# A new instruction order for a one-core attention and GEGLU block, with three of four normalised inputs taken from a transposed copy in DRAM

## The chip, the core and the metric

The kernel runs on one core of a Trainium2 chip. A core has five instruction streams: TensorE (matrix products and transposes; PE in the profile, its weight loads PEld), VectorE (DVE), ScalarE (ACT), GpSimd (POOL) and SyncE (SP), which here issues nearly all DMA transfers. Each stream runs its instructions in the order in which they were written. TensorE writes to PSUM, eight banks of 128 partitions by 512 fp32; VectorE and ScalarE read and write PSUM and SBUF; GpSimd works on SBUF alone. The metric is the device time of one execution in microseconds, median of the runs; lower is better.

## The reference

The input is 2048 tokens of width 512, in four segments of 512 tokens. First comes attention with a compressive memory, 32 heads of width 16, and then a gated feed-forward block of inner width 1376 (cut):

```python
h  = x + _A_ref(_layernorm(x), wq, wk, wv, wo, beta)
h2 = h + _B_ref(_layernorm(h), w_gate, w_up, w_down)
# _A_ref, per head, over the segments s = 0..3:
logits = qs @ ks.T * scale + mask       
a_dot  = softmax(logits) @ vs
a_mem  = phi(qs) @ M / (phi(qs) @ z + 1e-6)   # phi(t) = t+1 if t>0 else exp(t)
o      = g * a_mem + (1 - g) * a_dot     # g = sigmoid(beta)
M, z   = M + phi(ks).T @ vs, z + phi(ks).sum()
# _B_ref
h = gelu(x @ w_gate) * (x @ w_up);  out = h @ w_down
```

The mask is `(ar[:, None] < ar[None, :]) * -1e9` over the 512 positions of a segment. All arithmetic is fp32.

## The kernel before

**Precision.** An fp32 product is made of three products of a fast format: each operand is split into a high and a low part (`split_weight`, `split_wv`, `split_psum`), where ScalarE copies the high part and VectorE or GpSimd subtracts it for the low one, and TensorE forms high by high, high by low and low by high (`SPLIT`).

**The first norm.** `ln1_first` handles segment 0. `ln1(s)` handles segments 1 to 3: it loads four tiles `rows[t]` of 128 tokens by 512 features (line 938) and calls `layer_norm` (736). There the mean and variance of each token come from VectorE (segment 1: `bn_stats`, 761) or ScalarE (segments 2 and 3: two passes with accumulators, 747 and 756). From them follow two factors per token, y (one over the standard deviation) and b (minus mean times y), four columns of 128 tokens each. For segment 1 they come from ScalarE's square root and VectorE's reciprocal (795 to 803), for segments 2 and 3 and the second norm from a short chain of VectorE operations on four columns (809, 811, 814; all of `steps` are recorded at line 778). Then ScalarE normalises the rows in place (805, 818). As projections need features on the partitions, TensorE transposes the rows, 32 instructions of 64 by 64 in two tilings per segment (831, by `sides`, 552, with a small VectorE copy "tock" at 564 between its two phases), and `split_psum` takes the result out of the banks in two parts (ScalarE 867, VectorE 868). The result is `XT[s]`, four pairs of 128 features by 512 tokens.

**Attention.** Work goes in 16 units of eight heads and one segment (`UNITS`: units 0 and 1 are of segment 0, 2 and 3 of segment 1, and so on). `qkv` projects q and k (`project`, 959; `project_first`, 980) and v (`vproj`, 1008 and 1021); transfers scatter q and k to the tiles `stq` and `stk` (1083, 1089). `pass_a` forms scores (1213), and VectorE takes their largest per query under the mask (1223). `pass_b` forms them again, transposed (1271); ScalarE takes the exponential (1277), GpSimd clears what is above the diagonal (1285), and TensorE multiplies by v (1299). `mem` reads the memory (1161, 1181), and `mup` adds to it (1124). `wo_seg` projects the output (1372, 1379).

**Feed-forward.** `ffn` runs the gate and up products by a seven-product scheme over blocks of the normed input (1563), with the gate's function in `geglu` (1581 to 1599). The down product runs transposed with seven products per pair of blocks for most of the inner width (`down7`, 1737 and 1748), and plainly for the rest (`down`, 1631 and 1639). `turned` transposes the first sort through DRAM (718, 722, 1774) and adds them up on GpSimd (1775). In pass 1 `geglu` splits the last whole block, f = 9, on VectorE (1599), other blocks of the plain sort on GpSimd. The very last `down` group of pass 1 writes the output; one of its tiles (s = 1, t = 3) is done in two halves of 256 columns, whose transfers go out on two queues.

**Order.** The instructions are not issued where the functions stand. Each call of `pe`, `act`, `dve`, `pool` or `dma` records an operation (a group of instructions of one engine) with a duration. `Sched.run` walks a list of operation numbers, `ORDER`, found beforehand by a search that used the same durations. It emits each operation in turn, and while it does so keeps a clock per engine, from which it knows at what time buffers come free: a `Pool_` hands out the buffer that has been free longest. So `ORDER` sets the order on every engine, and the durations in the code set only which of several free buffers or banks is given out. All eight PSUM banks form one pool (`banks`, 567).

Of the kernel before, what the change touches and what calls it, by code (L numbers as in the profile page):

```python
# [15 lines left out]
P = 128  # L16
D = 512
# [397 lines left out]
class Sched:  # L415
# [7 lines left out]
    def op(self, eng, dur, prio, fn, ins=(), outs=(), acq=(), lat=None, chain=False,  # L423
# [18 lines left out]
        for v in o.vals:  # L442
            v.users += 1
# [61 lines left out]
def infini_geglu(ctx: ExitStack, tc: tile.TileContext, x, wq, wk, wv, wo, beta,  # L505
# [220 lines left out]
    def layer_norm(prio, rows, dst, off=False, keep=None, acq=None, done=(), behind=(), scratch=None, by_side=False, swap=None):  # L726
# [57 lines left out]
        def z_():  # L784
            return z.t
# [1096 lines left out]
```

## Time and profile before

| | |
|---|---|
| Median of 3 runs | 741.16 us (741.01 to 743.85) |
| The profiled execution: its time, its span | 740.42 us, 738.7 us |
| TensorE clock granted | 1.000 |
| Busy in the span: PE, DVE, ACT, POOL | 719.6, 634.8, 534.0, 523.1 us |
| DMA | 137.32 MB in 100798 packets, mean 186 GB/s |
| First attention products to the last ones | about 24 to 390 us |
| Gate, up and down products | about 390 to 734 us |

A busy time is the union of an engine's instructions; in the two-tile modes of attention several matrix instructions run side by side, so the sum of their durations is larger. A line of a group gives line, engine, operation, what it writes and reads, count, busy time and mean length of one in ns, and then the idle time of the engine just before, with what ended it. In a timeline a row gives start and length in us. In the chain of waits the rows are pieces of the path that ended last.

### The profile page before, as it was taken

What the parts mean: (1) busy time and instruction counts of PE and PEld (TensorE: products, weight loads), DVE (VectorE), ACT (ScalarE), POOL (GpSimd) and SP (SyncE); (2) the same over time, 40 slices, a digit from 0 to 9 for tenths busy, and PEclk for the clock granted to TensorE, in tenths of its full rate; (3) what the DMA queues carried; (4) which work ended last, traced back from release to release, by engine and by line L of the source; (5) the groups of instructions that cost most, each with busy time, mean ns of one, the idle gap of its engine ahead of it and who ended that gap; (6) DMA issues with size and microseconds to landing.
All of it is one profiled execution on the core that took longest, in us unless ns stands there. A gap on an engine that the chain in (4) does not pass through costs nothing.

```text
span 738.7 us, 19243 instructions
## 1 busy us (share of the span) xinstructions
PE 719.6 (97%) x6442; PEld 570.6 (77%) x6442; DVE 634.8 (86%) x1990; ACT 534.0 (72%) x1138; POOL 523.1 (71%) x815
## 2 busy tenths in 40 slices
PE   6999999999999999999999999999999999999996
PEld 5877877777878787777666888888887778888885
DVE  6998889988988888898987665889999999779996
ACT  6789979798685878867867656978787665666341
POOL 6344253554553746778899899998999977698766
PEclk9999999999999999999999999999999999999999
DMA  7754537656666776887856267677574249756767
GB/s 256 204 144 109 131 99 191 183 142 174 170 157 168 193 202 190 210 237 202 212 189 211 74 198 234 214 238 216 185 219 142 71 127 269 247 180 204 220 173 248
DMA packets 100798, 137.32 MB, mean 186 GB/s; under 512 B 18028, under 2 KB 40732, under 8 KB 100700
## 3 DMA queue, kind: packets, MB, share of 16 engines
q1 hardware_dynamic: 100396, 135.71, 63.6%
q8 instruction: 51, 0.84, 0.5%
q10 hardware_dynamic: 304, 0.39, 0.2%
q14 instruction: 47, 0.39, 0.2%
HBM read 70.67 MB, written 39.26 MB: 149 GB/s over the span
## 4 chain that ended last, share of the span: by engine, by line
PE 67%; DVE 11%; issue 3%; POOL 2%; DMA 2%; ACT 2%; SPq 1%; ACTq 0%; DVEq 0%; POOLq 0%
PE bank L1563 23%; PE bank L959 8%; PE bank L1299 7%; PE bank L1737 7%; PE bank L1271 5%; PE bank L1213 4%; PE bank L1379 3%; PE bank L1372 3%; PE bank L1008 3%; DVE row L1748 2%; DVE aside L1223 2%; PE bank L1631 2%; DVE bank L1223 1%; PE bank L1181 1%; DMA t_dram<-row 1%
## 5 line engine op out<-in xcount | busy, mean ns | idle before, releaser
L1277 ACT ACTIVATE row<-bank 128x512 f32<-128x512 f32 x320 | 170.9, 608 | 24.8 <-PE bank L1271 20.3
L1285 POOL TENSOR_SCALAR_AFFINE_SELECT row<-row 128x256 f32<-128x256 f32 (+1 forms) x320 | 107.8, 364 | 96.1 <-ACT row L1277 95.0
L1223 DVE CUSTOM_DVE_ANT_0 aside<-bank,amask 128x256 f32<-128x256 f32 (+2 forms) x384 | 141.1, 419 | 12.4 <-PE bank L1213 6.7
L959 PE MATMUL bank<-slot,slot 64*128 64x512 f32 x720 | 113.5, 403 | 0.3 <-DVE nm L1223 0.2
L1563 PE MATMUL bank<-slot,slot 128*128 128x512 f32 (+1 forms) x366 | 97.3, 390 | 0.0
L1223 DVE CUSTOM_DVE_ANT_0 bank<-bank,amask 128x512 f32<-128x512 f32 x128 | 86.1, 710 | 10.5 <-PE bank L1213 7.5
L1271 PE MATMUL bank<-stq,stk 64*128 64x128 f32 (+3 forms) x512 | 82.1, 337 | 0.8 <-ACT row L1114 0.5
L1299 PE MATMUL bank<-row,vaug 128*32 128x512 f32 (+3 forms) x1024 | 79.0, 436 | 1.8 <-DVE nm L1223 1.2
L1213 PE MATMUL bank<-stk,stq 64*128 64x256 f32 (+3 forms) x512 | 78.9, 326 | 1.7 <-DVE nm L1223 1.1
L1563 PEld LDWEIGHTS bank<-slot,slot 128*128 128x128 f32 (+1 forms) x366 | 67.8, 186 | 15.8 <-ACT stq L1419 0.4
L1748 DVE TENSOR_TENSOR row<-row,bank 128x512 f32<-128x512 f32 x110 | 72.0, 677 | 7.1 <-PE bank L1737 5.6
L959 PEld LDWEIGHTS bank<-slot,slot 64*128 64x128 f32 x720 | 73.3, 185 | 6.0 <-DVE nm L1223 0.7
L1528 POOL TENSOR_TENSOR slot<-row,slot 128x512 fp32r<-128x512 f32 (+3 forms) x60 | 67.1, 1124 | 14.1 <-ACT slot L1526 14.0
L1271 PEld LDWEIGHTS bank<-stq,stk 64*128 64x128 f32 x512 | 55.5, 185 | 15.5 <-DVE nm L1223 3.7
L1213 PEld LDWEIGHTS bank<-stk,stq 64*128 64x128 f32 x512 | 56.1, 185 | 9.6 <-DVE nm L1223 2.4
L1737 PE MATMUL bank<-slot,half 128*128 128x512 f32 x234 | 61.7, 390 | 0.0
L1299 PEld LDWEIGHTS bank<-row,vaug 128*32 128x32 f32 x1024 | 30.0, 109 | 39.2 <-issue 34.1
L1008 PE MATMUL bank<-slot,slot 64*128 64x256 f32 x672 | 53.4, 284 | 0.0
L1570 ACT ACTIVATE vaug<-bank 128x512 f32<-128x512 f32 (+1 forms) x66 | 38.5, 591 | 18.6 <-PE bank L1563 18.5
L1737 PEld LDWEIGHTS bank<-slot,half 128*128 128x128 f32 x234 | 43.8, 188 | 9.6 <-DVE row L1748 0.4
L1223 DVE DVE_READ_ACCUMULATOR2_ANT nm<- 128x1 f32 x512 | 49.9, 97 | 0.0
L1008 PEld LDWEIGHTS bank<-slot,slot 64*128 64x128 f32 x672 | 48.7, 186 | 1.0 <-DVE mb L1138 0.2
(228 smaller groups left out, 1722.2 us busy)
## 6 DMA issues: line engine op xcount, KB each, us to landing
stq<-slot SPq DMA_DIRECT2D x96, 128.0 KB
stk<-slot SPq DMA_DIRECT2D x94, 128.0 KB
row<-x SPq DMA_DIRECT2D x32, 256.0 KB
pv_dram<-row SPq DMA_DIRECT2D x32, 256.0 KB
row<-r_dram SPq DMA_DIRECT2D x28, 256.0 KB
wd_dram<-half SPq DMA_DIRECT2D x28, 256.0 KB
half<-wd_dram SPq DMA_DIRECT2D x28, 256.0 KB
row<-wu SPq DMA_DIRECT2D x20, 256.0 KB
```

The source lines that it names most:

```text
L959: return nc.tensor.matmul(pm[i].t, w[i].t[rows_of(r), wi, dc * P:(dc + 1) * P], XT[s][dc].t[rows_of(r), xi, :], start=(dc, wi, xi, ph) == ...
L1008: return nc.tensor.matmul(pms[n].t[:, 256 * t:256 * t + 256], XT[s][dc].t[rows_of(r), xi, t0:t0 + P], whl[wi].t[rows_of(r), dc // 2, 256 * ...
L1213: nc.tensor.matmul(sa.t[:, c0:c0 + w], sq.t[own, p, i * P:(i + 1) * P], sk.t[own, p, 0:w], start=True, stop=True, tile_position=(64 * a, 0 ...
L1223: nc.vector.tensor_tensor_reduce(out=(sa.t[:, c0:c0 + w] if i > 2 else aside[:, turns[0]:turns[0] + w]), in0=sa.t[:, c0:c0 + w], in1=amask ...
L1271: nc.tensor.matmul(sc.t[:, c0:c0 + D - q0], sk.t[own, p, q0:q0 + P], sq.t[own, p, q0:D], start=True, stop=True, tile_position=(64 * a, 0), ...
L1277: act(w, prio, lambda sc=sc, e=e: nc.scalar.activation(e.t[:, :w], sc.t[:, :w], AF.Exp), [sc, vtab], [e])
L1285: nc.gpsimd.affine_select(v, v, pattern=pat + [[1, P]], compare_op=OP.is_ge, fill=0.0, base=0, channel_multiplier=-1)
L1299: nc.tensor.matmul(pv.t[32 * n:32 * n + 32, kb * P:D], va.t[:, 136 * kb + 17 * j:136 * kb + 17 * j + 32], e.t[:, lo:lo + D - kb * P], star ...
L1528: pool(0.14 + 2.13e-3 * (hi - lo), prio, lambda: nc.gpsimd.tensor_tensor(v.t[:, 1, :hi - lo], r.t[:, lo:hi], v.t[:, 0, :hi - lo].bitcast(F ...
L1563: nc.tensor.matmul(dst.t[:w], v.t[:, wi, c0 + j * w:c0 + (j + 1) * w], b[bk][j].t[:, xi, :], start=first and j == 0 and n == 0, stop=j == ...
L1737: nc.tensor.matmul(dst[u].t, ws[a].t[0][:, wi, P * u:P * u + P], h[bk].t[:, xi], start=first and m == 0, stop=m == 2, skip_group_check=True)
L1748: dve(D, prio, lambda u=u, acc=acc: nc.vector.tensor_tensor(acc.t, acc.t, src[u].t, op=OP.add), [src[u]], [acc])
```

## The change

**A new list.** `ORDER` is replaced throughout; it has 5322 entries in place of 5308.

**Turns.** The planner's clock gets a rule for banks: where ScalarE and VectorE both read one bank, one starts only after the other has ended. It enters the planned times, and nothing is emitted for it.

**The first norm of segments 1 to 3.** `layer_norm` is called with `seg=s` and, once y and b are there, calls the new `across`. y and b (4 columns of 128 tokens) are written to a small DRAM tensor as 512 single elements each; after both have landed, each is read back as one row of 512 spread over all 128 partitions. A transposed copy of x, which the host lays out as one more input, is loaded in four tiles of 128 features by 512 tokens. GpSimd multiplies each by the first factor row and adds the second, ScalarE copies the high part, and GpSimd subtracts for the low part. The normalising pass of ScalarE, the transposes, "tock" and `split_psum` of these segments go. The rows are still loaded, for mean and variance.

**Small parts.** In the chain of four-column operations the value z is kept in the bank that holds the other scratch values, with one added copy to SBUF, for every norm with scratch; two planned durations change with it. For the block f = 9 `geglu` writes its product into a bank that it has just read, and the two halves of its split are read from there. The split of the last output tile into two halves is undone.

```diff
@@ Op recording and Sched.run
+        o.reads = [v for v in ins if v.pool is not None and v.pool.turns] if eng in ("ACT", "DVE") else []
...
+            for v in o.reads:
+                for e, end in v.read.items():
+                    if e != o.eng:
+                        at = max(at, end + LAT[e][o.eng])
...
+            for v in o.reads:
+                v.read[o.eng] = end
@@ infini_geglu
-    PD = PX = PYZ = PA = PB = PPV = Pool_(banks)
+    PD = PX = PYZ = PA = PB = PPV = Pool_(banks, turns=True)
...
+    n_dram = dram.tile([NSEG, 2, D], F32, name="n_dram")
@@ layer_norm
         def z_():
-            return z.t
+            return sc.t[:, 12:16] if scratch else z.t
+
+        def third():
+            if scratch:
+                nc.vector.tensor_copy(z.t, z_())
+            nc.vector.scalar_tensor_tensor(u_(), z.t, -10.0 / 3.0, z_(), op0=OP.add, op1=OP.mult)
...
-            dve(280, prio, inv, [z, mv], [y, b])
-            for t in range(4):
+            dve(910, prio, inv, [z, mv], [y, b])
+            for t in range(4) if seg is None else []:
...
+        if seg is not None:
+            return across(prio, seg, y, b, dst)
@@ new
+    def across(prio, s, y, b, dst):
+        vn, ab = Val(), [Val(PROW), Val(PROW)]
+        for i, v in enumerate((y, b)):
+            dma(prio, lambda i=i, v=v: nc.sync.dma_start(n_dram[s, i].rearrange("(t p) -> p t", p=P), v.t),
+                [v], [vn], kb=100, dur=0.5, chain=True)
+        for i, r in enumerate(ab):
+            src = n_dram[s, i]
+            dma(prio, lambda src=src, r=r: nc.sync.dma_start(r.t, bass.AP(
+                tensor=src.tensor, offset=src.offset, ap=[[0, P], [1, D]])), [vn], [r])
+        for dc in range(ND):
+            r = Val(PROW)
+            dma(prio, lambda dc=dc, r=r: nc.sync.dma_start(r.t, xt_in[s * ND + dc]), [], [r])
+            for i, o in enumerate((OP.mult, OP.add)):
+                pool(1.24, prio, lambda i=i, o=o, r=r: nc.gpsimd.tensor_tensor(r.t, r.t, ab[i].t, op=o), [ab[i]], [r])
+            act(D, prio, lambda dc=dc, r=r: nc.scalar.activation(dst[dc].t[:, 0], r.t, AF.Copy), [r], [dst[dc]],
+                src=0.092)
+            pool(1.24, prio, lambda dc=dc, r=r: nc.gpsimd.tensor_tensor(
+                dst[dc].t[:, 1], r.t, dst[dc].t[:, 0].bitcast(F32), op=OP.subtract), [r], [dst[dc]])
@@ geglu
+            if f == 9 and hh:
+                o = g_ if s else u_
...
-            act(D, prio, lambda: nc.scalar.activation(hh.t[:w, 0], e.t[:w], AF.Copy), [e], [hh],
-                src=0.09)
+            act(D, prio, lambda: nc.scalar.activation(hh.t[:w, 0], o.t[:w], AF.Copy), [o], [hh],
+                src=0.067 if f == 9 else 0.09)
...
-                hh.t[:w, 1], e.t[:w], hh.t[:w, 0].bitcast(F32), op=OP.subtract), [e], [hh])
+                hh.t[:w, 1], o.t[:w], hh.t[:w, 0].bitcast(F32), op=OP.subtract), [o], [hh])
@@ down
-                parts = 2 if (p, fl, s, t) == (1, groups[-1], 1, 3) else 1
...
+                a = ACC[4 * s + t]
+                pm = Val(PD)
```

More of the change, by code (lines that the diff above doesn't have):

```diff
@@ L58, with __init__ @@
 ORDER = [
[271 rows of a table removed]
[271 rows of a table added]
 ]
 class Pool_:
-    def __init__(self, tiles, fifo=False, then=None):
+    def __init__(self, tiles, fifo=False, then=None, turns=False):
+        self.turns = turns
         self.free = [(0.0, i, t) for i, t in enumerate(tiles)]
@@ L391, in __init__ @@
         self.users = 0
+        self.read = {}
         self.until = 0.0
@@ L399 @@
     __slots__ = ("eng", "dur", "lat", "fn", "prio", "vals", "preds", "succ", "n", "ready", "idx", "head", "tail",
-                 "mode")
+                 "mode", "reads")
 LAT = {
@@ L505, in infini_geglu @@
 def infini_geglu(ctx: ExitStack, tc: tile.TileContext, x, wq, wk, wv, wo, beta,
-                 wg, wu, wd, wdp, out):
+                 wg, wu, wd, xt_in, wdp, out):
     nc = tc.nc
@@ L724, in blocks_out, with layer_norm @@
                     q.t[32 * a:32 * a + 32].rearrange("p (b x) -> p b x", b=4)), [q], [v], kb=70, dur=0.5, chain=True)
-    def layer_norm(prio, rows, dst, off=False, keep=None, acq=None, done=(), behind=(), scratch=None, by_side=False, swap=None):
+    def layer_norm(prio, rows, dst, off=False, keep=None, acq=None, done=(), behind=(), scratch=None, by_side=False, swap=None, seg=None):
         bn, mv = Val(PBN), Val(PMV)
@@ L784, in z_ @@
         def z_():
-            return z.t
+            return sc.t[:, 12:16] if scratch else z.t
[3 more added lines that the diff above has]
+            nc.vector.scalar_tensor_tensor(u_(), z.t, -10.0 / 3.0, z_(), op0=OP.add, op1=OP.mult)
         steps = [(stt(u_, v_, 1.0, y_, OP.mult, OP.mult), [v, y], [u]),
-                 (stt(z_, u_, 1.0, y_, OP.mult, OP.mult), [u, y], [z]),
-                 (stt(u_, z_, -10.0 / 3.0, z_, OP.add, OP.mult), [z], [u]),
+                 (stt(z_, u_, 1.0, y_, OP.mult, OP.mult), [u, y], [sc if scratch else z]),
+                 (third, [sc], [u, z]) if scratch else (third, [z], [u]),
                  (stt(y_, u_, 5.0, y_, OP.add, OP.mult), [u, y], [y]),
@@ L810, in layer_norm @@
             for f, ins, outs in steps:
-                dve(4, prio, f, ins, outs)
+                dve(200 if f is third and scratch else 4, prio, f, ins, outs)
         if off:
@@ L940, in ln1 @@
         layer_norm(prio, rows, XT[s], off=s > 1, done=[Val()] if s < 2 else [],
-                   behind=[*XT[0], *XL] if s == 1 else [], scratch=PPV if s < 2 else PD, by_side=True)
+                   behind=[*XT[0], *XL] if s == 1 else [], scratch=PPV if s < 2 else PD, by_side=True, seg=s)
         if s < 2:
@@ L1590, in geglu @@
             o = g_ if s and f % 2 and by7(p, f) else e
+            if f == 9 and hh:
+                o = g_ if s else u_
             dve(D, prio, lambda: nc.vector.scalar_tensor_tensor(
-                o.t[:w], r.t[:w], 0.5, u_.t[:w], op0=OP.mult, op1=OP.mult), [u_] if o is r else [u_, r], [o])
+                o.t[:w], r.t[:w], 0.5, u_.t[:w], op0=OP.mult, op1=OP.mult), [v for v in (u_, r) if v is not o], [o])
             HH[p, f, s] = hh or o
@@ L1620, in down, with dn @@
             for t in range(4):
-                parts = 2 if (p, fl, s, t) == (1, groups[-1], 1, 3) else 1
-                a, W_ = ACC[4 * s + t], D // parts
-                halves = [slice(i * W_, (i + 1) * W_) for i in range(parts)]
-                pms = [Val(PD) for _ in halves]
+                a = ACC[4 * s + t]
+                pm = Val(PD)
                 for f in fl:
-                    def dn(t=t, f=f, s=s, pm=None, cs=None):
+                    def dn(t=t, f=f, s=s, pm=pm):
                         w = FW[f]
@@ L1630, in dn @@
                         for n, (hi, wi) in enumerate(SPLIT):
-                            nc.tensor.matmul(pm.t[:, cs], HH[p, f, s].t[:w, hi, t * P:(t + 1) * P],
-                                             v.t[:w, wi, cs], start=f == fl[0] and n == 0,
+                            nc.tensor.matmul(pm.t, HH[p, f, s].t[:w, hi, t * P:(t + 1) * P],
+                                             v.t[:w, wi, :], start=f == fl[0] and n == 0,
                                              stop=f == fl[-1] and n == 2)
-                    for pm, cs in zip(pms, halves):
-                        pe(3 * mm(W_), prio, lambda dn=dn, pm=pm, cs=cs: dn(pm=pm, cs=cs),
-                           [HH[p, f, s], FWS[p, f]["d"]], [pm])
-                for i, (pm, cs) in enumerate(zip(pms, halves)):
-                    to = Val(PC) if parts > 1 else a
-                    dve(W_, prio, lambda a=a, pm=pm, cs=cs, to=to: nc.vector.tensor_tensor(
-                        to.t[:, cs], a.t[:, cs], pm.t[:, cs], op=OP.add), [pm, a], [to])
-                    if fl in ((10,), (8, 9)):
-                        n, q = 8 * p + 4 * s + t, nc.scalar if i else nc.sync
-                        dst = g_dram[n * P:n * P + P] if fl == (10,) else tokens(out, p, s, t, cs)
-                        dma(prio, lambda to=to, cs=cs, q=q, dst=dst: q.dma_start(
-                            dst, to.t[:, cs]), [to], [GD[n]] if fl == (10,) else [])
+                    pe(3 * mm(D), prio, dn, [HH[p, f, s], FWS[p, f]["d"]], [pm])
+                dve(D, prio, lambda a=a, pm=pm: nc.vector.tensor_tensor(a.t, a.t, pm.t, op=OP.add), [pm], [a])
+                if fl in ((10,), (8, 9)):
+                    n = 8 * p + 4 * s + t
+                    dst = (g_dram if fl == (10,) else out)[n * P:n * P + P]
+                    dma(prio, lambda a=a, dst=dst: nc.sync.dma_start(dst, a.t), [a],
+                        [GD[n]] if fl == (10,) else [])
     def tokens(x, p, s, t, cs=slice(0, D)):
@@ L1870 @@
         "wd": np.ascontiguousarray(np.asarray(inputs["B_w_down"])),
+        "xt": np.ascontiguousarray(np.asarray(inputs["A_x"]).reshape(NSEG, D, ND, P).transpose(0, 2, 3, 1).reshape(
+            NSEG * ND, P, D)),
         "wdp": np.ascontiguousarray(np.asarray(inputs["B_w_down"])[:2 * BY7[0] * P].reshape(-1, 4, 2, 2, 32).transpose(
```

542 rows, old and new, of the table ORDER are left out of this document.

## Prediction

> **What bounds the kernel now.** I read the totals and the chain of waits first, then the busy time of each engine by stage, then the groups of instructions that the diff touches.
>
> ```profile
> span 738.7 us, 19243 instructions
> PE 719.6 (97%) x6442; PEld 570.6 (77%) x6442; DVE 634.8 (86%) x1990; ACT 534.0 (72%) x1138; POOL 523.1 (71%) x815
> PE 67%; DVE 11%; issue 3%; POOL 2%; DMA 2%; ACT 2%; SPq 1%; ACTq 0%; DVEq 0%; POOLq 0%
> ```
>
> ```profile
> core 0: us, PE busy (x) PEld busy (x) DVE busy (x) ACT busy (x) POOL busy (x), PEclk, DMA share, GB/s
> ...
> 24.00:60.00 36.00, 35.21 (x445) 29.52 (x447) 33.89 (x161) 30.39 (x73) 14.86 (x37) 1.00 0.57 155
> ...
> 146.00:182.00 36.00, 35.68 (x454) 26.67 (x447) 30.99 (x130) 31.25 (x72) 19.38 (x52) 1.00 0.59 158
> 24.00:390.00 366.00, 359.92 (x4793) 278.64 (x4793) 322.46 (x1371) 294.67 (x660) 208.06 (x469) 1.00 0.65 174
> 390.00:700.00 310.00, 309.53 (x1381) 250.52 (x1378) 264.26 (x503) 213.16 (x425) 273.48 (x290) 1.00 0.62 192
> 700.00:738.70 38.70, 32.91 (x148) 26.36 (x146) 31.34 (x71) 10.67 (x18) 25.46 (x21) 1.00 0.71 216
> ```
>
> From the chain of waits, one piece of the feed-forward stage:
>
> ```profile
> 402.37 12.32 PE bank L1563 x54
> ```
>
> From 390 to 700 us TensorE idles 0.5 us of 310, and a 512-column product takes 12.32 / 54 = 0.228 us, a steady cadence. No order makes this stage shorter; the change neither adds nor removes a product there. So what the change can win lies in attention (24 to 390 us), where TensorE idles 366 - 359.9 = 6.1 us, VectorE is busy 88% (94% from 24 to 60 us) and ScalarE 81%, and in the last 39 us. In attention TensorE and VectorE must both lose work for the time to fall. GpSimd has 158 us free there.
>
> **What the change removes and adds.** The rows of the work that segments 1 to 3 lose, and of a GpSimd operation of the kind that they gain:
>
> ```profile
> L831 PE MATMUL bank<-ident,row 64*128 64x64 f32 x160 | 10.5, 229 | 0.7 <-DVE row L822 0.5
> L868 DVE TENSOR_TENSOR slot<-bank,slot 128x512 fp32r<-128x512 f32 x17 | 11.1, 683 | 0.0
> L867 ACT ACTIVATE slot<-bank 128x512 fp32r<-128x512 f32 x17 | 9.8, 624 | 0.0
> L564 DVE COPY tock<-bank 128x1 f32<-128x1 f32 x48 | 7.4, 155 | 6.1 <-PE bank L1181 2.7 <-PE bank L959 2.1 <-PE bank L831 0.5
> L805 ACT ACTIVATE row<-row,ln,ln x4: 797/809/817, 23.4 to 26.6; 128x512 f32<-128x512 f32 x4
> L818 ACT ACTIVATE row<-row,ln,ln 128x512 f32<-128x512 f32 x16 | 12.8, 816 | 0.2 <-DVE ln L814 0.2
> L1338 POOL TENSOR_TENSOR row<-row,row 128x512 f32<-128x512 f32 x16 | 20.6, 1291 | 3.9 <-DMA row<-r_dram 3.9
> ```
>
> The 160 transposes serve five norms of 32; three go: 96 / 160 x 10.5 = **6.3 us of TensorE**. VectorE loses 12 x 0.683 + 6 x 0.155 = 9.1 us. ScalarE loses the normalising pass, 4 x 0.81 + 8 x 0.816 = 9.8 us; its 12 copies of 0.624 us stay, with a row as source. GpSimd gains 36 operations of 1.291 us, **46.5 us**. SP's queue gains 24 transfers: 12 loads of x and 6 spreads of 256 KB, and 6 writes of 512 single elements. All three engines that are nearly full in attention shed work, so I count TensorE's 6.3 us in full, **-6.3**. The bounds: -9.1 where VectorE sets the pace, 0 where the transposes only filled a wait of TensorE.
>
> **The order.** It is a new list throughout: of 1215 TensorE groups only some 150 keep their neighbour. Its "turns" change only the time that the planner assigns, and so which bank or buffer is handed out; no instruction gets a wait from them. What can be counted in the lists: changes between the tilings of TensorE (row halves, column quarters, whole) fall from 91 to 83, four visits fewer to the column tiling. What a visit costs is bounded by one with nearly no columns in it:
>
> ```profile
> 129.08 0.46 PE L1124 MATMUL bank<-vaug,row 128*32 128x34 f32 x32
> 129.47 0.46 PE L831 MATMUL bank<-ident,row 64*128 64x64 f32 x8
> ```
>
> 0.39 us from start to start, columns included, so four visits are worth 0 to 1.6 us; I take -0.8. For the rest of the reordering the trace gives bounds only: it can at best win the 6.1 us of idle TensorE and might lose as much; I take 0 and keep both ends.
>
> **Short operations that wait for GpSimd.** The norm's step that multiplied z by z from two SBUF operands, beside the same step with a bank operand; then three pieces at 380 and 728 us:
>
> ```profile
> L778 DVE SCALAR_TENSOR_TENSOR bank<-bank,ln 128x4 f32<-128x4 f32 x18 | 3.0, 168 | 0.4
> L778 DVE SCALAR_TENSOR_TENSOR bank<-ln 128x4 f32<-128x4 f32 x6 | 2.5, 419 | 0.2
> ```
>
> ```profile
> 380.41 1.18 DVE bank L778
> ```
>
> ```profile
> 727.01 0.75 DVE L1639 TENSOR_TENSOR row<-row,bank 128x256 f32<-128x256 f32 x2 [0.46 <-POOL row L1775]
> 728.89 1.38 DVE L1599 TENSOR_TENSOR slot<-row,slot 128x512 fp32r<-128x512 f32 x1 [1.13 <-ACT slot L1596]
> 730.32 3.25 PE L1631 MATMUL bank<-stq,slot 128*128 128x512 f32 x13 [0.63 <-DVE slot L1599]
> 732.32 2.05 DVE L1639 TENSOR_TENSOR row<-row,bank 128x512 f32<-128x512 f32 x3 [0.26 <-PE bank L1631]
> ```
>
> Four elements take 0.168 us with a bank operand, 0.419 on average without, and 1.18 at 380 us, on the chain. There the change saves 1.18 - 0.17 less the copy that it adds (0.17 by the same row): **-0.8**. The copy costs the five other norms about as much as it saves. At 728.89 the last subtraction reads two SBUF operands and takes 1.38 us; TensorE waits for it. From a bank it takes 0.68 (the L868 row): **-0.7**. Undoing the split of one output tile costs nothing: its halves ran at 727.0, and three whole tiles follow at 732.3, where the end hangs; were it last in the new list, half an addition (0.34) would come back. The new list ends in a GpSimd addition and one output tile, as the old one does.
>
> [...]
>
> **The new wait: the factors of segment 1.** Today:
>
> ```profile
> 0.00:20.00 20.00, 13.68 (x98) 11.69 (x99) 13.69 (x38) 12.12 (x31) 13.60 (x32) 1.00 0.69 241
> ```
>
> ```profile
> 19.56 2.03 SPq L1083 DMA_DIRECT2D stq<-slot  x3
> ```
>
> ```profile
> 21.93 0.53 DVE L802 SCALAR_TENSOR_TENSOR ln<-mv,ln 128x4 f32<-128x4 f32 x1
> ```
>
> ```profile
> 34.14 1.70 PE L1008 MATMUL bank<-slot,slot 64*128 64x256 f32 x23
> ```
>
> The factors are there at 22.5 us, and the first product with segment 1 starts at 34.1: 11.7 us. In the new list the last of its rows is SP's 12th transfer, not the 16th: 4 x 262 KB at 241 GB/s, 4.4 us earlier. Then follow a write, a spread back, and ten GpSimd operations up to the first half that a product needs, 12.9 us. No row shows a transfer of single elements; the nearest are steps of the chain:
>
> ```profile
> 702.80 2.01 DMA out_dram<-row
> ...
> 717.20 4.19 DMA row<-y_dram
> ```
>
> ```profile
> 542.94 4.76 DMA t_dram<-row
> ```
>
> So 2.0 to 4.8 us each way: 4.0 + 12.9 - 4.4 - 11.7 = +0.8 us to 9.6 + 12.9 - 4.4 - 11.7 = +6.4 us. I take **+2**: the write is 2 KB, nearer to 2.0, the spread 256 KB, 3 or so. Behind the spread that waits for both writes SP holds the three scatters of the first query tile (19.56 us today), so the first pass of scores can start later by the write's landing, up to 4.8 us; the list covers that with four groups of the next projection, moved ahead of it. Segments 2 and 3 write their factors over a hundred TensorE groups ahead; 0.
>
> [...]
>
> **The sum**, against the profiled execution's own 740.4 us: -6.3 - 0.8 - 0.8 - 0.7 + 2 = -6.6, so 733.8; the median of the runs is 741.16, 0.7 above, so **734.5 us**.
>
> **Rivals.**
> (1) *The new order also wins the idle time.* If TensorE's 6.1 us of idling in attention go as well: 728.4. For it: VectorE's 9.1 us fall where it is fullest. Against: in the stages with little idling TensorE is already at its cadence. 0.19.
> (2) *The gain is hidden.* The factors' chain takes its upper end (+6.4 in place of +2) and the transposes only filled waits for VectorE's masks and ScalarE's exponentials, half of the 6.3 lost: 734.5 + 4.4 + 3.2 = 742. To it belongs the case that the list is better only in the planner's account, which neither its turns nor its other prices make true on the chip. For it: 94% of VectorE at 24 to 60 us. 0.20.
> (3) *Slower: GpSimd becomes the bound.* Its queue is in order, and it has to clip each exponential before the products with v.
>
> ```profile
> POOL row L1285 <- ACT row L1277: 13.5, 7, 3.5
> ```
>
> This is what it waited from 146 to 182 us, about where the list puts the twelve operations of segment 3 (261st to 331st TensorE group): 19.4 + 15.5 = 34.9 of 36 us busy. If the long operations cannot use those waits, clips come late, and the products after them. The gain of 6.6 is spent once the 36 operations cost TensorE 6.6 / 36 = 0.18 us each; at a third of their length, 0.43, it is +15.5 - 6.6: 750. Against it: 158 us of free GpSimd in attention, and clips that stand in the list ahead of their product by several groups. 0.14.
>
> Forecast 0.47: 731 to 738. What a measurement here tells from no change is about 0.5%, 3.7 us. Faster by more than that: nearly all of the forecast and rival 1, 0.65; within: rival 2 and the forecast's edge, 0.21; slower: 0.14. The range reaches over rivals 1 and 2 and the cheaper end of 3: 726 to 744.
>
> **What would show it.** L831 down to 64 transposes; TensorE's busy time in attention down by about 6 us with idling no greater; the step at 380 us at 0.2 us and the last subtraction at 0.7; the first product with segment 1 by 36 us. Wrong it would be with a GpSimd wait of TensorE or of the clips' products that grew beyond 6 us, or a first product with segment 1 after 40 us.

## Result: slower, 761.4 us, and the profile after

The changed kernel takes **761.36 us** (median; 760.17 to 763.39), the kernel before 741.09 beside it: a ratio of **1.0265 [1.0243, 1.0286]**, 20 us slower. The forecast was 734.5, in a range of 726 to 744. The profiled execution took 763.4 us. From its page, the span, the busy times and TensorE's clock in 40 slices of 19 us:

```profile
span 761.6 us, 19104 instructions
PE 721.0 (95%) x6340; PEld 575.7 (76%) x6340; DVE 626.9 (82%) x1977; ACT 524.3 (69%) x1126; POOL 565.2 (74%) x851
PEclk9779989799999999999999999999999999999999
```

TensorE does 102 matrix instructions fewer than before and is busy 1.4 us longer, and its clock, 9 tenths or more in every slice before, is down to 7 or 8 tenths in four of the first eight slices. The stretches that the prediction quoted, now (us, busy us of each engine with its count, clock, DMA share, GB/s):

```profile
24.00:60.00 36.00, 24.83 (x260) 21.01 (x260) 19.53 (x95) 18.54 (x49) 20.78 (x30) 0.76 0.64 174
...
24.00:390.00 366.00, 337.31 (x4434) 263.59 (x4432) 295.16 (x1280) 270.49 (x612) 227.00 (x463) 0.95 0.67 175
390.00:700.00 310.00, 309.23 (x1534) 249.72 (x1531) 263.32 (x547) 218.89 (x444) 279.75 (x317) 1.00 0.62 191
```

The feed-forward stage has its old cadence. Between 24 and 390 us TensorE stands for 28.7 us where it stood for 6.1. Where, its timeline shows (start, length, line, operation; in brackets the idle time before and what ended it):

```profile
23.21 3.01 PE L995 MATMUL bank<-slot,slot 64*128 64x512 f32 x24
35.58 1.22 PE L1249 MATMUL bank<-stk,stq 64*128 64x256 f32 x8 [9.36 <-DMA stq<-slot]
...
47.05 2.12 PE L1044 MATMUL bank<-slot,slot 64*128 64x256 f32 x12 [0.23 <-DVE nm L1259]
...
93.10 0.44 PE L1249 MATMUL bank<-stk,stq 64*128 64x384 f32 x2 [1.94 <-issue]
...
95.96 0.29 PE L1280 MATMUL bank<-ident,mm 64*32 64x64 f32 x2 [1.61 <-ACT row L1313]
...
147.23 0.79 PE L1249 MATMUL bank<-stk,stq 64*128 64x256 f32 x4 [8.21 <-issue]
...
163.93 0.72 PE L1160 MATMUL bank<-vaug,row 128*32 128x34 f32 x14 [2.77 <-issue]
```

Five stops, together 23.9 us. Each lies behind a write of factors (L883, issued at 17.7 us for segment 1, 82.5 and 83.9 for segment 2, 132.8 and 154.7 for segment 3). SP's queue shows the first:

```profile
17.71 1.27 SPq L883 DMA_DIRECT2D n_dram<-ln  x2
19.03 0.98 SPq L891 DMA_DIRECT2D row<-xt  x2
29.07 0.33 SPq L887 DMA_DIRECT2D row<-n_dram  x1
29.51 1.31 SPq L1119 DMA_DIRECT2D stq<-slot  x2
```

The spread (L887) waits for the two writes of 2 KB from 20.0 to 29.1 us; the scatters of the first query tile stand behind it, and the first scores behind those. Later segments wait in another form. SP's waits (us in total, times, longest):

```profile
SPq L1363 <- DMA pv_dram<-row: 15.8, 3, 10.2
SPq L887 <- DMA n_dram<-ln: 9.0, 1, 9.0
SPq L1363 <- DMA n_dram<-ln: 6.8, 1, 6.8
```

L1363 has nothing to do with the norm: it fetches attention's products, and the 256 KB transfer that it waits for was issued just behind a factor write. The transfers around a factor write are held up too: from 20 to 24 us, with two loads of 256 KB of x issued (L891), the core moves 16 GB/s.

### The profile page after: what moved, and what is told of

It is laid out like the page before. It is cut to its first block, busy times and chain, and to the rows that moved or that the text cites. A ratio compares the mean times of both kernels' runs of the same rounds, so it can differ in the third digit from the quotient of the medians.

```text
span 761.6 us, 19104 instructions
## 1 busy us (share of the span) xinstructions
PE 721.0 (95%) x6340; PEld 575.7 (76%) x6340; DVE 626.9 (82%) x1977; ACT 524.3 (69%) x1126; POOL 565.2 (74%) x851
## 5 line engine op out<-in xcount | busy, mean ns | idle before, releaser
L995 PE MATMUL bank<-slot,slot 64*128 64x512 f32 x720 | 117.5, 415 | 0.0
L1249 PE MATMUL bank<-stk,stq 64*128 64x256 f32 (+3 forms) x512 | 83.2, 339 | 22.1 <-issue 10.1
L1599 PE MATMUL bank<-slot,slot 128*128 128x512 f32 (+1 forms) x387 | 102.8, 390 | 0.0
L1599 PEld LDWEIGHTS bank<-slot,slot 128*128 128x128 f32 (+1 forms) x387 | 71.8, 186 | 16.2 <-issue 0.3
L1249 PEld LDWEIGHTS bank<-stk,stq 64*128 64x128 f32 x512 | 57.7, 192 | 34.3 <-issue 22.0
L995 PEld LDWEIGHTS bank<-slot,slot 64*128 64x128 f32 x720 | 77.7, 193 | 5.8 <-DVE nm L1259 0.2
L1307 PE MATMUL bank<-stq,stk 64*128 64x384 f32 (+3 forms) x512 | 81.8, 337 | 0.2
L1564 POOL TENSOR_TENSOR slot<-row,slot 128x512 fp32r<-128x512 f32 (+3 forms) x60 | 68.9, 1155 | 9.9 <-ACT slot L1562 6.2
L1767 PE MATMUL bank<-slot,half 128*128 128x512 f32 x288 | 75.7, 389 | 0.0
L1767 PEld LDWEIGHTS bank<-slot,half 128*128 128x128 f32 x288 | 54.1, 188 | 11.3
L1044 PEld LDWEIGHTS bank<-slot,slot 64*128 64x128 f32 x672 | 48.0, 192 | 1.3 <-DVE nm L1259 0.6
```

The source lines that it names most:

```text
L995: return nc.tensor.matmul(pm[i].t, w[i].t[rows_of(r), wi, dc * P:(dc + 1) * P], XT[s][dc].t[rows_of(r), xi, :], start=(dc, wi, xi, ph) == ...
L1044: return nc.tensor.matmul(pms[n].t[:, 256 * t:256 * t + 256], XT[s][dc].t[rows_of(r), xi, t0:t0 + P], whl[wi].t[rows_of(r), dc // 2, 256 * ...
L1249: nc.tensor.matmul(sa.t[:, c0:c0 + w], sq.t[own, p, i * P:(i + 1) * P], sk.t[own, p, 0:w], start=True, stop=True, tile_position=(64 * a, 0 ...
L1307: nc.tensor.matmul(sc.t[:, c0:c0 + D - q0], sk.t[own, p, q0:q0 + P], sq.t[own, p, q0:D], start=True, stop=True, tile_position=(64 * a, 0), ...
L1564: pool(0.14 + 2.13e-3 * (hi - lo), prio, lambda: nc.gpsimd.tensor_tensor(v.t[:, 1, :hi - lo], r.t[:, lo:hi], v.t[:, 0, :hi - lo].bitcast(F ...
L1599: nc.tensor.matmul(dst.t[:w], v.t[:, wi, c0 + j * w:c0 + (j + 1) * w], b[bk][j].t[:, xi, :], start=first and j == 0 and n == 0, stop=j == ...
```

## Experiments

Theories, written ahead of the runs: **W**, each element-wise write (one whose pieces are single elements of 4 bytes) holds up the DMA transfers of the core (its "DMA rings") for about 10 us; **G**, the 36 added GpSimd operations are the loss (the prediction's rival 3); **O**, the new order itself is worse.

**1. Longer runs in the write.** VectorE turns the factors first, and one transfer writes both in runs of 128 bytes (128 runs, 16 KB, of which 32 runs hold the factors):

```
-  nc.sync.dma_start(n_dram[s, i].rearrange("(t p) -> p t", p=P), v.t)       # twice, 512 x 4 B
+  nc.vector.tensor_copy(fac[:, 0:4], y.t); nc.vector.tensor_copy(fac[:, 4:8], b.t)
+  nc.vector.transpose(fact, fac)
+  nc.sync.dma_start(n_dram[s].rearrange("c (i q) -> i c q", q=32), fact)    # once
```

> The changed kernel, but the factors of segments 1 to 3 go to DRAM in one transfer of 32 runs of 128 bytes (VectorE turns them round first in two copies and a transpose) instead of two transfers of 512 single elements each. Theory W (the element-wise writes): each pair holds the DMA rings for about 10 us, SP's queue stands behind it, TensorE stops for some 24 us in all and then works at a halved clock for a while. W expects 731 to 740 us, about 1.4% below the changed kernel's profiled 763 less its 24 us: no stop of TensorE over 2 us after segments 1 to 3, a mean granted clock above 0.99. Rival G (36 more GpSimd operations) and rival O (the new order itself) both expect 755 to 764, with the stops still there.

Measured: **732.74 us**, 0.9896 [0.9845, 0.9948] of the kernel before. SP's queue, GpSimd and TensorE in its timeline, then the busy times of its page and its window of 24 to 60 us:

```profile
18.00 0.67 SPq L899 DMA_DIRECT2D n_dram<-fact  x1
...
20.06 0.33 SPq L908 DMA_DIRECT2D row<-n_dram  x1
```

```profile
25.08 9.94 POOL L914 TENSOR_TENSOR row<-row,row 128x512 f32<-128x512 f32 x8 [1.91 <-DMA row<-n_dram]
...
35.43 5.00 POOL L917 TENSOR_TENSOR slot<-row,slot 128x512 fp32r<-128x512 f32 x4
```

```profile
26.58 0.74 PE L1270 MATMUL bank<-stk,stq 64*128 64x256 f32 x8 [0.62 <-DMA stq<-slot]
...
37.59 0.58 PE L1065 MATMUL bank<-slot,slot 64*128 64x256 f32 x1
```

```profile
PE 715.3 (98%) x6340; PEld 570.5 (78%) x6340; DVE 626.8 (86%) x1987; ACT 524.7 (72%) x1126; POOL 565.2 (77%) x851
```

```profile
24.00:60.00 36.00, 33.43 (x358) 26.61 (x356) 27.17 (x132) 25.22 (x64) 25.34 (x40) 0.91 0.69 195
```

The write lands within 2.1 us, the 9.36 us stop is 0.62, up to 24 us the core moves 250 GB/s in place of the changed kernel's 200, and the first product with segment 1 comes 9.5 us earlier than in the changed kernel. With the same list and the same GpSimd work the loss is gone: G and O fall as its cause. Against this run the changed kernel's span is 30.6 us longer: for the same 6340 instructions TensorE is busy 5.8 us longer, at a mean clock of 0.977 against 0.994, and it stands 24.8 us longer.

**2. Runs of 16 bytes.** The factors in token order, `"(p t) -> p t"`, two transfers of 128 runs; GpSimd reads them back with a stride.

> The changed kernel, but the factors are written in token order, 128 runs of 16 bytes a transfer instead of 512 of 4, two transfers as before; GpSimd reads the factors back with a stride. W with a price per run: a quarter of the stops, 740 to 748 us. W with a price per transfer whatever its runs: 755 to 764. G and O: 755 to 764, or more, if the strided reading makes the 24 GpSimd operations longer.

Measured: **737.34 us**, 0.9938 [0.9917, 0.9958]. SP's queue:

```profile
17.51 0.93 SPq L883 DMA_DIRECT2D n_dram<-ln  x2
...
20.82 0.33 SPq L887 DMA_DIRECT2D row<-n_dram  x1
```

Two writes as before, and the spread goes out 3.3 us after them instead of 11.4: the price is not one of a transfer. The time is below both ranges of the expectation, so a price per run, a quarter of the stops, is too high as well. With the stride GpSimd is busy 257.9 us between 24 and 390 us, 254.0 in run 1; how much of the 4.6 us over run 1 that makes isn't separated.

**3. No GpSimd work.** `pool(1.24, prio, lambda: None, [ab[i]], [r])` in place of the 24 multiplications and additions, so segments 1 to 3 aren't normalised.

> The changed kernel without the 24 multiplications and additions on GpSimd that apply the factors (so segments 1 to 3 go into the products without their normalisation); the writes, the spreads and the waits on them stay. W expects that the stops stay: 753 to 763 us. Rival G expects most of the loss back: 738 to 745 us.

Measured: **760.67 us**, 1.0256 [1.0211, 1.0300]. The first stop is still there, among TensorE's waits:

```profile
PE bank L1249 <- DMA stq<-slot: 8.7, 1, 8.7
```

**4. The writes alone, in the kernel before.**

```
+  for i in range(2) if Q in (8, 14) else []:      # ahead of the transfer of attention's products
+      nc.sync.dma_start(n_dram[i + 2 * (Q > 8)].rearrange(
+          "(t p) -> p t" if Q == 8 else "(p t) -> p t", p=P), gt[:, i])
```

> The kernel before, with four transfers that nobody waits for or reads: two of 512 single elements ahead of the transfer of the attention's products at about 132 us, two of 128 runs of 16 bytes ahead of another one later. W expects that the transfer behind the first pair lands some 10 us later, that TensorE stops there for several us and its clock falls after it: 748 to 762 us. At the second pair a stop of a quarter of that or none. G and O, and a write that costs no more than its 2 KB: 739 to 743 us.

Measured: **750.06 us**, 1.0106 [1.0069, 1.0143]: 8.9 us by the medians for four writes of 2 KB that nobody reads, two element-wise and two in runs of 16 bytes. The element-wise pair was issued at 150.6 us, the other at 227.5. Windows behind each, and TensorE's timeline:

```profile
154.00:158.00 4.00, 4.00 (x46) 3.65 (x44) 2.07 (x6) 3.23 (x9) 3.99 (x11) 1.00 1.12 19
158.00:164.00 6.00, 0.41 (x6) 0.19 (x2) 0.72 (x4) 0.34 (x2) 1.04 (x5) 0.76 0.52 47
230.00:234.00 4.00, 3.29 (x52) 2.83 (x44) 2.70 (x12) 0.98 (x4) 0.78 (x3) 1.00 0.32 93
```

```profile
164.31 1.07 PE L1272 MATMUL bank<-stq,stk 64*128 64x256 f32 x4 [5.89 <-ACT row L1115]
```

The two columns at the end show it: a DMA share of 1.12 while 19 GB/s move, so by the profile the DMA engines are taken and carry next to nothing. The share is no sure sign, though: in the changed kernel, from 20 to 28 us, it is 0.25 with 30 GB/s. Behind the 16-byte pair 93 GB/s move, and TensorE's longest stop there is 0.71 us; run 6, which has the element-wise pair alone, costs as much as all four writes.

**5. Forms of the element-wise write, one execution of each**, in the kernel before, unread, four in a kernel at about 86, 150 to 156, 188 to 195 and 240 to 247 us. The first kernel's:

```
+  runs = {2: n_dram[0, 0:4, :].rearrange("t p -> p t"),
+          8: n_dram[1, :, 0:16].rearrange("(t p) q -> p t q", p=P)[:, :, 0],
+          12: n_dram[2].rearrange("(t p) q -> p t q", p=P)[:, :, 0],
+          16: n_dram[3, 0].rearrange("(t p) -> p t", p=P)}
```

> The kernel before with four transfers that nobody waits for, each ahead of a transfer of the attention's products, far apart in time: 512 elements of 4 bytes that lie side by side in DRAM; 512 elements 64 bytes apart; 512 elements 512 bytes apart; 128 elements side by side. If the price is one of descriptors (so many runs, whatever their place), the first three hold the rings alike, 8 to 11 us each, the fourth a quarter: 755 to 775 us. If it is one of neighbouring elements written into the same stretch of DRAM, only the first and fourth hold them: 743 to 755 us.

The second form did not become what the expectation says: the rows of this tensor are 512 bytes long, so its elements lie as far apart as the third's. Measured: 749.41 us in one run. Windows that begin 1 to 5 us behind each write:

```profile
88.00:92.00 4.00, 3.55 (x56) 3.26 (x54) 1.83 (x11) 2.46 (x7) 0.20 (x1) 1.00 1.04 41
157.00:160.00 3.00, 3.00 (x32) 2.80 (x30) 1.77 (x9) 2.68 (x7) 1.46 (x6) 1.00 0.62 181
197.00:201.00 4.00, 3.02 (x49) 2.80 (x47) 3.98 (x16) 2.73 (x9) 2.45 (x8) 1.00 0.67 147
252.00:256.00 4.00, 3.79 (x48) 1.81 (x44) 3.34 (x14) 3.29 (x7) 2.29 (x3) 1.00 0.56 36
```

Elements side by side hold the rings (41 and 36 GB/s), as many elements 512 bytes apart don't (181 and 147 GB/s). A low rate alone is no hold: the kernel before moves 4 GB/s from 154 to 158 us, with TensorE busy throughout. What counts is that work waits: behind the first write TensorE stands 3.87 us, and behind the fourth, of 128 elements, SP waits 4.6 us for a transfer of 16 KB (L1194 for r_dram, 1.0 in the kernel before). So it isn't the number of pieces, which is 512 in each of the first three forms. What the hold comes from is the question of the next two kernels. The second kernel's writes lie 64, 16, 32 and 128 bytes apart; the third's as its expectation says:

```
+  nc.sync.dma_start(bass.AP(tensor=base.tensor, offset=base.offset + start, ap=[[p, P], [t, 4], [1, 1]]), ...)
```

> The kernel before with four unread writes of 512 single elements at the same four places, which differ in how far apart the elements lie in DRAM: 64, 16, 32 and 128 bytes, in order of time. In the run of the four forms the second one's elements lay 512 bytes apart (the row of its tensor was 512 bytes long), not 64, so the distance from which elements don't hold the rings is open. If it is a stretch of 64 bytes that they must share, the second and third hold the rings (a DMA share near or above 1 with some 40 GB/s behind them), the first and fourth don't: 745 to 755 us. If every distance under 512 bytes holds them, all four do: 755 to 775 us.

> The kernel before with four unread writes of 512 single elements at the same four places. In the run of the distances nothing held, from 16 bytes apart on. [...] In order of time: elements side by side with a partition's four next to each other (16 bytes a partition); 16 bytes apart but begun 32 bytes later; 8 bytes apart; 8 bytes apart and begun 32 bytes later. [...] If it comes from nearness alone, the first holds, and the third and fourth alike.

Measured: 741.52 and 746.30 us in one run each. The same windows of the two:

```profile
87.00:91.00 4.00, 3.96 (x62) 3.68 (x61) 3.85 (x22) 3.60 (x11) 0.71 (x3) 1.00 0.76 197
150.00:153.00 3.00, 3.00 (x33) 2.70 (x30) 2.12 (x10) 2.68 (x7) 1.45 (x5) 1.00 0.78 176
189.00:193.00 4.00, 4.00 (x63) 3.84 (x60) 3.87 (x16) 2.55 (x7) 3.05 (x10) 1.00 0.61 144
242.00:246.00 4.00, 4.00 (x42) 3.51 (x42) 3.50 (x18) 3.64 (x7) 3.47 (x8) 1.00 0.62 165
```

```profile
90.00:94.00 4.00, 2.71 (x38) 2.28 (x36) 1.05 (x8) 1.56 (x6) 0.00 (x0) 1.00 0.63 39
156.00:159.00 3.00, 3.00 (x30) 2.71 (x30) 1.81 (x10) 2.66 (x7) 1.44 (x6) 1.00 0.47 148
196.00:200.00 4.00, 2.92 (x46) 2.64 (x42) 3.87 (x17) 2.73 (x8) 2.41 (x8) 1.00 0.53 140
249.00:253.00 4.00, 4.00 (x44) 2.92 (x44) 3.56 (x19) 3.76 (x9) 3.13 (x8) 1.00 0.72 162
```

From 8 bytes apart on nothing holds, begun 32 bytes later or not (140 to 197 GB/s); directly adjacent elements do, in a partition's order too (39 GB/s). Both kernels write four times 512 pieces, and only the one with adjacent elements is slower (746.30 us against 740.84 beside it; the other 741.52 against 740.29): the number of pieces alone doesn't do it. Nor does the order of bytes alone, as the same order in runs of 16 bytes (run 4's second pair, 93 GB/s) makes no such hold. A stretch of 64 bytes that elements share falls as a cause (16 and 32 bytes apart: 176 and 144 GB/s), and so does nearness alone (8 bytes apart: 140 and 162). What adjacency does stays open.

**6. Another queue.** The element-wise pair of run 4 issued by ScalarE (`nc.scalar.dma_start`).

> The kernel before with the two element-wise dummy writes issued by ScalarE instead of SP, just ahead of the copy whose transfer they stood before in the run of the dummy writes. If the writes fill the DMA rings or engines that all queues share, SP's transfers stop as they did: 747 to 753 us. If only the queue that issued them stands: 740 to 743 us.

Measured: 750.09 us in one run. SP's waits from 150 to 162 us:

```profile
SPq L1175 <- DMA n_dram<-gt: 7.9, 1, 7.9
```

The profile has a transfer of SP wait 7.9 us for writes that ScalarE issued; TensorE stands 5.74 us, and the price is that of run 4. So what is held is shared by the two queues.

**7. TensorE kept busy in the first stop.** The changed kernel, with 72 unread products ahead of the projection that ends at 26.2 us:

```
+  for k in range(72) if warm and (dc, wi, xi, ph, i) == (0, 0, 0, 0, 0) else []:
+      nc.tensor.matmul(pm[k % 2].t, w[k % 2].t[...], XT[s][0].t[...], start=True, stop=True, ...)
```

> The changed kernel with 72 products that nobody reads ahead of the projection that TensorE does last before its first stop (26 to 35.6 us), so that it works on through most of the stop. If TensorE's clock is cut because it stood still, the clock stays at 1.00 up to 50 us (0.50 at 32 to 40 and 48 to 52 us in the changed kernel) and the kernel gets 2 to 5 us shorter: 756 to 760 us. If the clock falls for another reason, the time stays at 760 to 764.

Measured: 759.70 us, 1.0236 [1.0188, 1.0284], not told apart from the changed kernel's 1.0265.

```profile
24.00:60.00 36.00, 32.97 (x342) 26.04 (x344) 20.38 (x99) 19.60 (x52) 20.81 (x30) 0.91 0.71 189
```

```profile
45.92 2.13 PE L1051 MATMUL bank<-slot,slot 64*128 64x256 f32 x12 [0.23 <-DVE nm L1266]
```

The clock from 24 to 60 us rises from 0.76 to 0.91. From 32 to 40 us it is 1.00 where it was 0.51, so that cut came because TensorE stood. The second cut stays, against the expectation: from 48 to 52 us the clock is 0.50 in both, here behind stops of 0.50 us at most, close together (TensorE busy 6.1 of 8 us from 40 to 48). Run 1 has one like it: 0.91 from 24 to 60 us, with no stop there over 0.62 us and 33.4 of 36 us busy. And the first product with segment 1 comes only 1.1 us earlier: GpSimd, behind the late factors, is busy 7.9 of the 8 us from 40 to 48, VectorE all of them. By the medians filling this stop is worth 1.7 us, inside the intervals.

**8. The removed work put back**, beside the 128-byte runs and in the new order: first the 96 transposes alone, then also 12 subtractions on VectorE and 12 copies on ScalarE.

```
+  nc.tensor.transpose(pm[r2].t[:, 64 * t:64 * t + 64], ident[rows_of(r2)], ...)   # 16 in two projections of each segment
...
-  dve(..., nc.vector.scalar_tensor_tensor(hl.t[:, 1, cols], ...))
+  dve(..., [nc.vector.scalar_tensor_tensor(hl.t[:, 1, cols], ...) for _ in range(2 if s and i == 0 else 1)])
-  act(..., nc.scalar.activation(dst[dc].t[:, 0], r.t, AF.Copy))
+  act(..., [nc.scalar.activation(o, r.t, AF.Copy) for o in (dst[dc].t[:, 0],) * 2])
```

> The kernel of the 128-byte runs (732.7 us) with 96 transposes of 64 x 64 that nobody reads added back to TensorE, 16 at the head of two projections of each of segments 1 to 3. If TensorE sets the pace in attention, as my term of -6.3 us has it, they cost 5 to 7 us: 738 to 740 us. If VectorE and ScalarE set the pace there, they fall into waits: 733 to 735 us.

> The kernel of the 128-byte runs with all the removed work put back beside it, in the new order: the 96 transposes as before, 12 more subtractions of 128 x 512 on VectorE (0.69 us each) and 12 more copies of 128 x 512 on ScalarE (0.62 us each) in segments 1 to 3, none of them needed. If its gain of 8.5 us on the kernel before is the removed work, most of it goes: 738 to 742 us. If it is the new order, the time stays at 734 to 737 us.

Measured: **734.69 us**, 0.9917 [0.9887, 0.9947], and **744.48 us**, 1.0054 [1.0042, 1.0066]. The pages of both:

```profile
PE 719.0 (98%) x6436; PEld 575.7 (79%) x6436; DVE 626.4 (85%) x1987; ACT 525.5 (72%) x1126; POOL 565.1 (77%) x851
```

```profile
PE 721.5 (97%) x6436; PEld 573.3 (77%) x6436; DVE 634.8 (86%) x1999; ACT 532.9 (72%) x1138; POOL 565.4 (76%) x851
```

The transposes keep TensorE busy 3.7 us longer and cost 2.0 us by the medians, as in the second case of their expectation; the intervals of the two kernels overlap, so this price is not told apart from nothing. The work of VectorE and ScalarE, 8.4 and 7.4 us of busy time more, costs another 9.8, above what I expected (738 to 742). Of the 9.4 us by which the span grows in this second step, TensorE, with the same 6436 instructions, stands 6.9 us longer and is busy 2.5 longer. With all of it back, the kernel, which still has the added GpSimd operations and transfers, is 3.7 us slower than the kernel before: no sign that the order wins anything, though the order alone isn't measured. Where the two engines' work is put weighs in this price; it stands in chains that products wait for.

**9. Two small parts, and the turns, in the kernel before.** The step with z in a bank and the last subtraction from a bank; then `Pool_(banks, turns=True)` with its accounting alone.

> The kernel before with two of the small parts alone: the norm's step that multiplies z by z with z in a PSUM bank, and the last subtraction of the feed-forward from a bank. My sum has -0.8 and -0.7 for them: 739.0 to 740.5 us, the step at 380 us at 0.2 us and the last subtraction at 0.7. If they are hidden: 740.5 to 742.

> The kernel before with the planner's rule of turns alone (two engines that read one bank are planned one after the other), the order unchanged. It can only hand out other buffers: 740 to 742.5 us. If the turns themselves do something on the chip, it differs by over 3 us.

Measured: **740.52 us**, 1.0004 [0.9985, 1.0023], and **741.31 us**, 1.0003 [0.9984, 1.0022]. From the VectorE timeline of the first:

```profile
380.56 0.17 DVE L790 SCALAR_TENSOR_TENSOR bank<-ln,bank 128x4 f32<-128x4 f32 x1
...
730.97 0.69 DVE L1606 TENSOR_TENSOR slot<-bank,slot 128x512 fp32r<-128x512 f32 x1 [1.08 <-ACT slot L1603]
```

Both operations are as short as forecast (0.17 and 0.69 us, before 1.18 and 1.38). In the kernel before the first lay beside an addition of GpSimd and ended with it (380.41 to 381.58 us, the addition 380.27 to 381.55), the second beside others (GpSimd busy without a gap from 724.0 to 732.7). No time is seen for it: the interval leaves 1.1 us at most of the 1.5 forecast. The turns show no effect by themselves.

**10. Three variants that came out slower than run 1.** The 128-byte runs with the old order, the new operations put by hand where the old passes and transposes stood; with segment 1 normalised on chip as before, again by hand; and with segment 1's four low halves on VectorE.

> The kernel of the 128-byte runs (732.7 us) with the order of the kernel before: only the list differs, the operations of the three norms stand where the old passes, transposes and copies stood. If the gain of 8.5 us is what my sum had it from (96 transposes and the shorter VectorE and ScalarE work, whatever the order): 731 to 736 us. If it is the new order that wins: 738 to 744 us.

> The kernel of the 128-byte runs with segment 1 normalised and transposed on the chip as before; only segments 2 and 3 read x transposed, and only they send factors by DRAM. If the rest of the stop behind segment 1 (TensorE busy 33.4 us of 24 to 60 at a clock of 0.91, before 35.2 at 1.00) is the factors' chain, it goes, and 32 transposes (2.1 us) come back: 728 to 731 us. If the new list itself leaves TensorE idle there: 733 to 737 us.

> The kernel of the 128-byte runs with segment 1's four subtractions of the low halves on VectorE instead of GpSimd. If GpSimd's chain (8 operations from 25.1 us, then four subtractions up to 40.4) is what the first product with segment 1 waits for at 37.6 us, that product starts 1 to 3 us earlier and the kernel gains 0.5 to 2 us: 730.5 to 732.5. If VectorE, busy with the masks of the first scores there, takes the subtractions late: 732.5 to 735.

Measured: **786.33 us**, 1.0610 [1.0586, 1.0634]; **741.07 us**, 0.9998 [0.9984, 1.0011]; **737.50 us**, 0.9955 [0.9943, 0.9967]. The longest waits of TensorE, in the first:

```profile
PE bank L1356 <- POOL row L1342: 14.2, 4, 5.9
PE bank L1016 <- POOL slot L703: 9.7, 1, 9.7
PE bank L1301 <- POOL mm L1295: 8.1, 1, 8.1
```

24 to 60 us of the second, and the third's longest wait in attention:

```profile
24.00:60.00 36.00, 31.46 (x328) 24.17 (x329) 23.77 (x110) 21.36 (x54) 8.23 (x22) 0.81 0.50 140
```

```profile
PE bank L1066 <- DVE slot L918: 2.8, 1, 2.8
```

The first is no test of the old order: where I put the multiplications they wait for factors (10.4 us in four waits), while weights and clips stand behind them in GpSimd's list and TensorE waits for those (14.2 us for clips, 9.7 for a weight). It shows what a bad place for them costs, 54 us over the same operations in the new list: rival 3's mechanism, at a price far above the one I gave it. The second fits neither case of its expectation: TensorE stands 4.5 us of this window (2.6 in run 1), in many short waits, and the clock is lower (0.81 against 0.91); as this order, too, was made by hand, the cause isn't separated. In the third VectorE is late with the halves, as its expectation's second case says, but the time is above that case's range (732.5 to 735).

## Why the prediction was wrong

**The step that failed** is the factors' wait: "the write is 2 KB, nearer to 2.0, the spread 256 KB, 3 or so", with 4.8 us as its upper end. The two writes took 11.4 us (17.71 to 29.07), 9.4 more than taken, of the 10.9 us by which the first product with segment 1 was later than forecast (47.05 against 36.1). The spread, 4.6 us from issue to GpSimd's first operation, was mis-sized too, by 1.6. The bounds came from rows of long runs; the prediction said that no row showed a transfer of single elements, and then let the neighbours' time be the upper end. With 128-byte runs the same step holds: write 2.1 us, spread 5.0 (20.06 to 25.08), first product at 37.59 us against 36.1 forecast (34.1 + 2), inside the bounds of +0.8 to +6.4. In the whole time the form of these writes is worth 28.6 us (761.36 against 732.74), in a term that stood at +2.

**The cover that failed** with it: "the list covers that with four groups of the next projection". These end at 26.2 us, and the scatters behind the spread were issued at 29.5, so TensorE stood 9.36 us.

**"Segments 2 and 3 ...; 0"** failed by its reason. That the factors are early was right and beside the point: what was sent around them is waited for. The other four stops, 14.5 us, come from there; the last of them in the form of the first, with SP issuing nothing from 159.2 to 163.95 us, where the spread behind the write of 154.7 is next in its order. I had named the queues that the writes pass and never asked what they do to transfers that need nothing of them.

**The clock** stood in no term. In the changed kernel the lower clock (0.977 against 0.994) goes with 5.8 us more of busy TensorE than in the run with 128-byte runs. With the long stop it falls: 0.76 from 24 to 60 us around a stop of 9.36, 0.91 with that stop filled. With shorter ones the runs give no single picture: the clock is 0.59 from 98 to 102 us behind stops of 1.94 and 1.61 us, it falls to 0.50 behind stops of 0.50 us at most in run 7, and it stays at 1.00 from 164 to 168 us behind one of 2.77. How much standing brings a cut is not shown here.

**The upper end**, +6.4, came from the same rows of long runs: the first product was 12.9 us late (47.05 against 34.14). Nor would a price for each element have been right: in run 5 as many elements show no hold when they lie 8 bytes apart or more (140 to 197 GB/s behind them). Their size alone doesn't explain the hold either: the elements far apart are as small.

**Terms of the sum.** The transposes, -6.3 "in full": 2.0 when put back, by the medians. I took TensorE's end of the bounds, because it was at its cadence 98% of the time; the end that I named for VectorE, -9.1, was nearer, since all the removed work together is worth 11.7 us where run 8 put it. A TensorE that is 98% busy can still be made to stand longer by the engines that feed it (6.9 us in run 8). -0.8 and -0.7 for the short operations: lengths right, time not seen. The turns: 0, right. The order: 0 taken, no gain seen; together with what the change adds on GpSimd and SP it costs 3.7 (run 8). The four visits to the column tiling, -0.8, were not tried. Without the element-wise writes the kernel stands at 732.74, near the forecast of 734.5, but by errors that offset each other: a gain larger than taken (11.7), and costs larger too (3.7).

**The rivals.** Rival 3 had the right sign and the wrong mechanism: without 24 of the 36 operations the kernel stays at 760.67. Rival 1 doesn't apply. Rival 2 named both weak places, the factors' chain and transposes that partly filled waits, but its price for the chain was the same upper end, +6.4, and its time of 742 is 19 us too low.

**The tests** that I named. The transposes, in the changed kernel's groups of instructions:

```profile
L848 PE MATMUL bank<-ident,row 64*128 64x64 f32 x64 | 3.3, 227 | 0.0
```

64 are left, and in run 9 the short operations are short, as forecast. That TensorE idles no more in attention failed (28.7 us against 6.1), and "wrong it would be with ... a first product with segment 1 after 40 us" decided it: 47.05.

The version with 128-byte runs beats both kernels: 732.74 us.

## What to carry to other kernels

A write of single, directly adjacent elements to DRAM is not priced by its bytes (two of 2 KB took 11.4 us here, one of 16 KB in runs of 128 bytes 2.1): keep such a write off a path where others transfer, or turn the tile on chip first so that the runs are long (two copies and a transpose of VectorE replaced a hold of some 10 us). Where the trace has no row for a kind of transfer, the nearest rows are no upper bound (4.8 us here, where 11.4 came); ask also what stands behind it in the queue, and which other transfers it may hold up. And before work counts in full on the engine that looks full, put work of the other engines beside it: here 16 us of VectorE and ScalarE cost 9.8, and 3.7 of TensorE cost 2.0, by the medians and in the places where they were put.

## What was not expected of the hardware

- Two element-wise writes of 2 KB hold up nearly all transfers of the core for 8 to 11 us (11.4 until segment 1's pair has landed, 7.9 of wait in SP's queue for a pair that ScalarE issued). In windows of 4 us behind segment 1's pair and in runs 4 and 6, 13 to 45 GB/s move, at a DMA share anywhere from 0.11 to 1.12.
- Of the forms tried only directly adjacent single elements do so (36 to 41 GB/s behind them); 512 elements 8, 16, 32, 64, 128 or 512 bytes apart don't (140 to 197 GB/s), one execution of each form.
- TensorE's clock was cut after a stop of 9 us, and filling that stop with 72 unread products, which brought it from 0.76 to 0.91, won less than can be told from no change. It was also cut behind stops of 0.5 us and less that lay close together (0.50 from 48 to 52 us in run 7).
